# Uncut float32 scores for the first 14 head pairs, moved weight loads, and two orders of work instead of one, in a kernel of attention and a gated feed-forward layer

## The chip, the cores and the metric

The kernel runs on one core of a Trainium2 chip. The metric is device time in microseconds (us) of that core. The core has five queues that matter here: PE (TensorE, matmuls and weight loads), DVE (VectorE), ACT (ScalarE), POOL (GpSimd) and SP (SyncE, which here issues nearly all DMAs). Each runs its own instructions strictly in the order in which the program emits them, and waits at semaphores for the others.

## What is computed

Eight batches, twelve heads, 448 positions, head size 64. Attention with capped scores, then a feed-forward layer on its output with squared ReLU and a sigmoid gate.

```python
# attention, per head
scores = q @ k.T / sqrt(64)
scores = cap * tanh(scores / cap)
attn = exp(scores - max(scores))
attn = attn / (sum(attn) + 1e-9)
x = attn @ v                       # heads side by side: [8, 448, 768]
# feed-forward
x_prev = x shifted by one position
xk = mu_k * x + (1 - mu_k) * x_prev
xr = mu_r * x + (1 - mu_r) * x_prev
k = relu(xk @ w_k)                 # [8, 448, 1024]
v = k * k @ w_v
out = sigmoid(xr @ w_r) * v
```

The weights arrive as float64, in pairs of 32-bit words.

## The kernel before

**Two phases.** The first phase walks over the 48 head pairs (8 batches of 6 pairs) in 54 steps. The second walks over 28 chunks of 128 tokens and computes gate and output; it is nearly all matmuls (`chunk2`, L482, with `mm2`, L475). Only the first phase is touched by the change.

**A step of the first phase.** Step i does scores, tanh, exp and row sums (`red`, L255) of pair i, the product with the values (`V`, `values`, L234) of pair i-1, and the normalisation and mixing (`norm`, `mix_old`, `mix_new`, `x_high`, `x_low`) of pair i-2. Keys are cut in three groups of 128 (S0, S1, S2) and a rest of 64, which is done for two pairs at once in even steps (`L`, `tanhL`, `expL`, `redL`, `VL`). The row sums go through DRAM twice to be inverted and spread over partitions: `gather` (four small DMAs), `recip` on DVE, `rec_store` and `rec_load`; `norm` of the next step needs the result.

**Scores.** `scores` (L197) multiplies in three terms. `qk_high` rounds q and k to float32r on POOL, `qk_low` subtracts to get the rest, also float32r and on POOL (both at step i for pair i+2), and high*high, low*high and high*low are summed in PSUM. A float32 operand that is not cut is also possible: the rest of 64 keys (L216) and the product with the values (L241) use it; one float32 matmul is two matmul instructions in the trace. Score tiles have two buffers, so that a group waits until tanh has read the one before the last.

**Key products.** From step 7 on, each step has four places K (`kpart`, L323), with 7 key matmuls in each place of an even step and 5 in each of an odd step (`key_split`, L530), 48 in two steps. They need the mixed x of the pairs and the converted key weights. `relu` and `k_store` on ACT empty a finished group.

**Weights.** 44 pieces (16 of the key weight first) are loaded one per step (`weight_load`), and an extra one at `more` in steps 1, 3, 5, 7 and 9. ACT takes the absolute value at the end of the step (`weight_abs`), and in the next step DVE does five operations for each piece (`f`, `weight_rest`; L395 to L403), POOL adds (`weight_sum`, L410) and rounds, and DVE subtracts one step later (`weight_low`, L423, for pieces of the key weight).

**The order** is written out by hand, in one list for even and one for odd steps; a name in the list emits its instructions, so the list sets each engine's queue.

```python
EVEN = """gather load_v load_vl weight_load more weight_low S0 S1 V VL L S2 f f f f f weight_rest tanh0 exp0 red0
weight_sum tanh1 exp1 red1 norm recip rec_store K qk_high qk_low tanhL mix_old mix_new x_high x_low relu k_store
K expL redL relu k_store K K tanh2 exp2 red2 relu k_store weight_abs load_qk rec_load x_store weight_store"""
```

**The passage.** After step 48 the buffers of attention are freed, and the weights of the second phase (14 loads of `w_d`, L544, in three buffers) are loaded and cut while the last key products run.

## Time and profile before

| | us |
|---|---|
| median of 3 runs (lowest, highest) | 977.08 (975.99, 978.48) |
| profiled execution: its own time | 976.81 |
| profiled execution: span of instructions | 975.0 |
| PE busy | 931.0 (95%) |
| DVE busy | 633.5 (65%) |
| ACT busy | 487.8 (50%) |
| POOL busy | 291.7 (30%) |

Busy shares are means over stages that differ. Positions are us from the start of the span. In the slices of the span, PE is at six to eight tenths in the first three (75 us), and at nine or more in all but the last after that. The clock that TensorE was granted is written as a share of full speed: 1.00 is 2.4 GHz, and 0.5 is 1.2 GHz.

### The profile page before, as it was taken

To read this page: it belongs to the slowest core of one execution; us is meant where nothing else is said; L and a number is where in the kernel's file an instruction comes from. 1 tells how busy PE (TensorE), PEld (TensorE's weight loads), DVE (VectorE), ACT (ScalarE), POOL (GpSimd) and SP (SyncE) were. 2 spreads that over 40 slices of the span, in tenths; PEclk is the share of its full clock that TensorE was granted. 3 is DMA by queue.
4 is the path that set the end of the run, shared out by engine and by line. 5 is a ranking of instruction groups with operands and counts; after the bars stand their busy time and mean duration, and the time that the engine had idled before them with its cause. 6 is when DMAs were issued, how large, how long until landed. Compare 5 with 4: busy or idle time off the path is not lost.

```text
span 975.0 us, 14675 instructions
## 1 busy us (share of the span) xinstructions
PE 931.0 (95%) x5328; PEld 747.0 (77%) x5328; DVE 633.5 (65%) x1128; ACT 487.8 (50%) x578; POOL 291.7 (30%) x315
## 2 busy tenths in 40 slices
PE   6667899999999999999999999999999999999997
PEld 3224566666666666666667899999999999999997
DVE  5999887788877778776553685464464464465450
ACT  6767777887888888887773121221221221121120
POOL 4566565555555546554422300000000000000000
PEclk8778999999999999999999999999999999999999
DMA  4554555766766766664434752332232233233221
GB/s 156 160 155 150 181 159 184 220 209 193 217 185 192 222 201 191 199 191 147 142 125 146 251 156 84 87 109 80 83 108 83 82 109 90 73 109 93 71 71 36
DMA packets 124706, 138.88 MB, mean 142 GB/s; under 512 B 19664, under 2 KB 109776, under 8 KB 124624
## 3 DMA queue, kind: packets, MB, share of 16 engines
q1 hardware_dynamic: 115408, 123.16, 42.7%
q10 hardware_dynamic: 9216, 14.68, 4.0%
q8 instruction: 44, 0.72, 0.3%
q14 instruction: 38, 0.31, 0.1%
HBM read 92.64 MB, written 42.40 MB: 139 GB/s over the span
## 4 chain that ended last, share of the span: by engine, by line
PE 82%; DVE 9%; DMA 3%; ACT 3%; issue 1%; SPq 1%; POOL 1%; DVEq 0%; ACTq 0%; POOLq 0%
PE pvv L479 23%; PE kps L336 20%; PE pr L479 17%; PE pv L241 10%; PE s L204 9%; DVE r L257 2%; PE pv L250 2%; PE s L216 1%; DMA wst<-w_d 1%; ACT p L222 1%; DVE wt L395 1%; ACT p L232 1%; DMA sq<-r 1%; DVE wa L399 1%; ACT p_left L232 1%
## 5 line engine op out<-in xcount | busy, mean ns | idle before, releaser
L257 DVE TRANSPOSE_TENSOR_REDUCE r<-p 128x28 f32<-128x896 f32 x144 | 158.8, 1109 | 72.7 <-ACT p L232 72.0
L79 ACT CAST xh<-t 128x768 fp32r<-128x768 f32 x27 | 22.6, 837 | 309.5 <-DVE t L462 309.5
L222 ACT ACTIVATE p<-s,scl_t 128x896 f32<-128x896 f32 x144 | 143.3, 995 | 23.0 <-PE s L204 15.2
L232 ACT ACTIVATE p<-p,cap_t 128x896 f32<-128x896 f32 x144 | 150.0, 1042 | 3.9
L336 PE MATMUL kps<-xkh,wkh 128*128 128x448 f32 x384 | 143.5, 374 | 3.4 <-ACT ko L343 3.2
L494 DVE TENSOR_TENSOR o<-pvv,rsg 128x768 f32<-128x768 f32 (+1 forms) x29 | 27.0, 930 | 181.2 <-PE pvv L479 180.3
L336 PE MATMUL kps<-xkl,wkh 128*128 128x448 f32 x384 | 142.7, 372 | 0.2 <-POOL xkl L85 0.2
L336 PE MATMUL kps<-xkh,wkl 128*128 128x448 f32 x384 | 140.2, 365 | 0.0
L241 PE MATMUL pv<-p,rv 128*64 128x448 f32 x576 | 125.9, 574 | 2.0 <-DVE xk L301 2.0
L479 PE MATMUL pvv<-wvh,kl 128*128 128x384 f32 x448 | 115.0, 334 | 0.0
L479 PE MATMUL pvv<-wvh,kh 128*128 128x384 f32 x448 | 114.9, 334 | 0.0
L479 PE MATMUL pvv<-wvl,kh 128*128 128x384 f32 x448 | 114.9, 334 | 0.0
L85 POOL TENSOR_TENSOR qkl<-rqk,qkh 128x832 fp32r<-128x832 f32 x47 | 93.1, 1980 | 3.9
L204 PE MATMUL s<-qkh 64*128 64x448 f32 x288 | 65.2, 448 | 29.7 <-ACT p L222 20.1
L204 PEld LDWEIGHTS s<-qkh 64*128 64x128 f32 x288 | 27.8, 188 | 83.3 <-ACT p L222 31.6
L241 PEld LDWEIGHTS pv<-p,rv 128*64 128x64 f32 x576 | 38.7, 143 | 66.7 <-issue 56.4
L479 PE MATMUL pr<-wrh,xh 128*128 128x384 f32 x336 | 85.5, 335 | 1.7 <-POOL xh L75 1.0
L479 PE MATMUL pr<-wrh,xl 128*128 128x384 f32 x336 | 85.5, 335 | 1.0 <-DVE xl L470 1.0
L336 PEld LDWEIGHTS kps<-xkh,wkh 128*128 128x128 f32 x384 | 72.1, 188 | 18.2 <-ACT ko L343 6.8
L479 PE MATMUL pr<-wrl,xh 128*128 128x384 f32 x336 | 85.2, 334 | 0.0
L410 POOL TENSOR_TENSOR wsq<-wa,wsq 128x384 f32<-128x384 f32 x44 | 44.4, 1010 | 129.8 <-DVE wsq L403 113.2
L336 PEld LDWEIGHTS kps<-xkl,wkh 128*128 128x128 f32 x384 | 72.1, 188 | 12.8 <-issue 6.8
(75 smaller groups left out, 1552.0 us busy)
## 6 DMA issues: line engine op xcount, KB each, us to landing
rqk<-qk SPq DMA_DIRECT2D x47, 448.0 KB
k_d<-ko ACTq DMA_DIRECT2D x64, 224.0 KB
kr<-k_d SPq DMA_DIRECT2D x28, 512.0 KB
x_d<-x SPq DMA_DIRECT2D x48, 224.5 KB
r<-rec_d SPq DMA_DIRECT2D x96, 112.0 KB
out<-o SPq DMA_DIRECT2D x27, 384.0 KB
xc<-x_d SPq DMA_DIRECT2D x24, 387.0 KB
rv<-v SPq DMA_DIRECT2D x48, 192.0 KB
```

Of the source, the lines that this page charges most:

```text
L79: self.nc.scalar.copy(out, x)
L85: {"p": self.nc.gpsimd, "v": self.nc.vector}[e].tensor_sub(*a)
L204: nc.tensor.matmul(s[:, h, 0:S], qk[a][p, k], qk[b][p, 0:S], start=(n == 0), stop=(n == 2))
L222: self.nc.scalar.activation(p32, self.S.pop((i, g))[:, :, 0:S], AF.Tanh, scale=self.scl_t)
L232: self.nc.scalar.activation(p32, p32, AF.Exp, scale=1.0 if self.maxima else self.cap_t)
L241: nc.tensor.matmul(pv[p, 0:S], v[:, g, h, :], ph[:, h, :], start=(g == 0), stop=False)
L250: self.nc.tensor.matmul(self.PV[i + p][o, 0:S], v[HALF[p], h, :], ph[HALF[p], h, :], start=False, stop=True)
L257: self.nc.vector.tensor_reduce(out=r1[:, :, 3 if g == "L" else g], in_=self.P32[i, g].rearrange("p h (b k) -> p (h b) k", k=32), axis=mybi ...
L336: nc.tensor.matmul(self.kps[fc][:, 0:S], w, m[:, dc, :], start=first, stop=last)
L410: {"p": self.nc.gpsimd, "v": self.nc.vector}[e].tensor_add(sq, f(a), sq)
L479: self.nc.tensor.matmul(ps[:, m, 0:HN], a[:, c, :], w[:, c, m * HN:m * HN + HN], start=(c == 0 and part == 0), stop=(c == n - 1 and part = ...
L494: nc.vector.tensor_mul(o[:, q], pv[:, q, 0:HN], rs[:, q])
```

## The change

The scores of pairs 0 to 13 are computed from the loaded float32 q and k, in one term; `qk_high` and `qk_low` fall away for these pairs. The five extra weight pieces are loaded in steps 1, 7, 8, 9 and 10. There are four lists instead of two: one pair for steps 0 to 13 and one for the others. The number of key matmuls per place stays as it was (the constants `KE`, `KO`, `KT` have the old values). In the maxima path, which runs only for a large cap, the same terms are used. `raw` and `QK` are no longer popped, which moves no work, and there are assertions on the order of key products.

```diff
+RAW = 14
+SW = 14
+MORE = (1, 7, 8, 9, 10)
+KFIRST = 28
+KE, KO, KT = (7, 7, 7, 7), (5, 5, 5, 5), 8
...
-EVEN = """gather load_v load_vl weight_load more weight_low S0 S1 V VL L S2 f f f f f weight_rest tanh0 exp0 red0
-weight_sum tanh1 exp1 red1 norm recip rec_store K qk_high qk_low tanhL mix_old mix_new x_high x_low relu k_store
-K expL redL relu k_store K K tanh2 exp2 red2 relu k_store weight_abs load_qk rec_load x_store weight_store"""
-ODD = """gather load_v weight_load more weight_low S0 S1 V S2 f f f f f weight_rest tanh0 exp0 red0
-weight_sum tanh1 exp1 red1 norm recip rec_store K qk_high qk_low tanh2 mix_old mix_new x_high x_low relu k_store
-K exp2 red2 relu k_store K K relu k_store weight_abs load_qk rec_load x_store weight_store"""
+START_EVEN = """gather weight_load load_v load_vl more load_qk weight_low S0 S1 K V VL L weight_rest f norm f tanh0 exp0
+qk_high weight_sum tanh1 exp1 relu k_store f recip red0 qk_low tanhL K S2 mix_old mix_new x_high x_low red1
+tanh2 relu expL redL exp2 k_store K K red2 f f weight_abs relu k_store rec_store rec_load x_store
+weight_store"""
+START_ODD = """gather more load_qk load_v weight_load f f f S0 S1 V S2 f f weight_low K tanh0 relu exp0 norm red0
+weight_rest weight_sum tanh1 recip rec_store qk_high tanh2 mix_old mix_new x_high qk_low x_low k_store exp2 K
+red2 relu exp1 red1 k_store K K relu weight_abs k_store weight_store x_store rec_load"""
+EVEN = """weight_load gather load_vl load_v load_qk weight_rest weight_low f S0 S1 V VL L S2 f f tanh1 tanh0 exp1 exp0
+qk_high weight_sum norm recip x_store more K qk_low tanhL relu mix_old red1 mix_new x_high x_low k_store K
+expL relu tanh2 redL f f red0 exp2 red2 k_store K K relu k_store weight_abs rec_store rec_load weight_store"""
+ODD = """gather more weight_store load_v weight_load f weight_rest S0 S1 V S2 weight_low f K relu tanh0 k_store exp0
+red0 qk_high weight_sum tanh1 f norm f recip load_qk rec_store K exp1 red1 f tanh2 mix_old mix_new x_high
+qk_low x_low exp2 relu k_store weight_abs K K relu k_store red2 rec_load x_store"""
...
+    def factors(self, i):
+
+        if i < RAW:
+            return (self.raw[i],), ((0, 0),)
+        return self.QK[i], ((0, 0), (1, 0), (0, 1))
+
     def scores(self, i, g):
-        nc, qk = self.nc, self.QK[i]
+        nc = self.nc
+        qk, terms = self.factors(i)
         s = self.ps_s.tile([P, 2, 512], F32, name="s")
         k = slice(S + g * P, S + (g + 1) * P)
 
-        for n, (a, b) in enumerate(((0, 0), (1, 0), (0, 1))):
+        for n, (a, b) in enumerate(terms):
             for h, p in enumerate(HALF):
-                nc.tensor.matmul(s[:, h, 0:S], qk[a][p, k], qk[b][p, 0:S], start=(n == 0), stop=(n == 2))
-        if g == 2:
-            self.QK.pop(i)
+                nc.tensor.matmul(s[:, h, 0:S], qk[a][p, k], qk[b][p, 0:S], start=(n == 0), stop=(n == len(terms) - 1))
         self.S[i, g] = s
...
-        for op in (EVEN if even else ODD).split():
+        for op in ((START_EVEN if even else START_ODD) if i < SW else EVEN if even else ODD).split():
...
-                if 0 <= j < NPAIR:
+                if 0 <= j < NPAIR and not (j < RAW and op in ('qk_high', 'qk_low')):
                     getattr(self, name.get(op, op))(j, *g)
...
-                if i in (1, 3, 5, 7, 9):
+                for _ in range(MORE.count(i)):
                     self.weight_load()
...
             self.load_qk(0)
-            self.qk_high(0, "v")
-            self.qk_low(0, "v")
             self.consts(cpool)
             self.init_sums(cpool)
             self.load_qk(1)
-            self.qk_high(1)
-            self.qk_low(1)
             self.load_qk(2)
```

## Rows read from the trace of the kernel before

**Rows 1.** The page's busy time of the engines over the whole span: us, share, instructions.

```profile
PE 931.0 (95%) x5328; PEld 747.0 (77%) x5328; DVE 633.5 (65%) x1128; ACT 487.8 (50%) x578; POOL 291.7 (30%) x315
```

**Rows 2.** Busy time of each engine in seven stretches. Columns: the stretch, its length, then for each engine busy us and number of instructions, the granted TensorE clock, the DMA engines' busy share and GB/s. The bounds are starts of S0 on PE: of step 5, 6 and 7 (51.30, 64.80, 75.10), of step 8, 10, 12 and 14 (90.85, 114.84, 137.28, 158.60); 504.00 lies in step 47, 557.65 is the end of the last key product and 576.65 the start of the second chunk's gate products.

```profile
51.30:64.80 13.50, 7.61 (x30) 3.27 (x32) 12.34 (x22) 7.86 (x9) 7.66 (x10) 0.62 0.45 134
64.80:75.10 10.30, 6.84 (x48) 2.58 (x46) 9.84 (x17) 8.43 (x10) 6.72 (x7) 1.00 0.54 175
90.85:114.84 23.99, 21.31 (x125) 13.92 (x124) 21.41 (x36) 17.40 (x22) 14.51 (x18) 1.00 0.56 170
114.84:137.28 22.44, 21.71 (x125) 13.84 (x124) 19.91 (x32) 16.17 (x21) 12.56 (x16) 1.00 0.55 174
137.28:158.60 21.32, 21.28 (x127) 14.15 (x128) 17.85 (x30) 17.63 (x23) 13.11 (x13) 1.00 0.63 193
158.60:504.00 345.40, 345.24 (x2031) 226.49 (x2032) 256.62 (x409) 280.51 (x331) 182.12 (x189) 1.00 0.61 187
557.65:576.65 19.00, 16.25 (x89) 15.12 (x88) 15.59 (x25) 2.26 (x3) 4.48 (x4) 1.00 0.52 152
```

**Rows 3.** PE in order of time in an odd step of the steady stretch, from its S0 (255.52) to that of the next step (264.42). Columns: start, duration, instruction, count.

```profile
255.52 0.47 PE L204 MATMUL s<-qkh 64*128 64x448 f32 x2
...
256.94 2.48 PE L241 MATMUL pv<-p,rv 128*64 128x448 f32 x12
259.35 0.47 PE L204 MATMUL s<-qkh 64*128 64x448 f32 x2
...
260.16 0.47 PE L336 MATMUL kps<-xkh,wkh 128*128 128x448 f32 x1
...
264.42 0.47 PE L204 MATMUL s<-qkh 64*128 64x448 f32 x2
```

**Rows 4.** DVE in order of time in steps 4 and 5: the last weight piece of step 4, red0 and red1 of that step, norm, the three operations of recip (only the first shown), mix_new, redL, then weight_low for two pieces, a weight piece and two reds.

```profile
49.59 1.19 DVE L395 TENSOR_SCALAR wt<-wsq 128x384 f32<-128x384 f32 x1
...
52.87 2.10 DVE L257 TRANSPOSE_TENSOR_REDUCE r<-p 128x28 f32<-128x896 f32 x2
54.89 0.58 DVE L286 TENSOR_TENSOR x<-pv,r 128x448 f32<-128x448 f32 x1
55.40 0.59 DVE L270 TENSOR_REDUCE sr<-sq 32x28 f32<-32x448 f32 x1
...
56.51 0.64 DVE L301 SCALAR_TENSOR_TENSOR xk<-x,mu_k,pv 128x448 f32<-128x448 f32 x1
57.14 1.11 DVE L257 TRANSPOSE_TENSOR_REDUCE r<-p_left 128x28 f32<-128x896 f32 x1
...
60.15 0.98 DVE L423 TENSOR_TENSOR wkl<-wsq,wkh 128x384 fp32r<-128x384 f32 x2
61.05 0.35 DVE L395 TENSOR_SCALAR wt<-wsq 128x384 f32<-128x384 f32 x1
...
63.29 2.10 DVE L257 TRANSPOSE_TENSOR_REDUCE r<-p 128x28 f32<-128x896 f32 x2
```

**Rows 5.** DVE's instructions from 23.9 to 139.6 us, grouped by line: count, busy us and mean ns of one, then idle time before them and what ended it.

```profile
L257 DVE TRANSPOSE_TENSOR_REDUCE r<-p 128x28 f32<-128x896 f32 x31 | 33.5, 1100 | 6.8 <-ACT p L232 6.6
L395 DVE TENSOR_SCALAR wt<-wsq 128x384 f32<-128x384 f32 x15 | 12.2, 816 | 0.5
L423 DVE TENSOR_TENSOR wkl<-wsq,wkh 128x384 fp32r<-128x384 f32 x16 | 9.9, 641 | 0.0
...
L397 DVE TENSOR_SCALAR wa<-wt 128x384 uint32<-128x384 uint32 x15 | 6.4, 428 | 0.5
...
L257 DVE TRANSPOSE_TENSOR_REDUCE r<-p_left 128x28 f32<-128x896 f32 x5 | 5.6, 1114 | 1.0 <-ACT p_left L232 1.0
```

**Rows 6.** POOL: the page's group of qk_low over the whole span (count, busy us, mean ns, idle time before), and the instruction in order of time at the weight piece that stands first in rows 4.

```profile
L85 POOL TENSOR_TENSOR qkl<-rqk,qkh 128x832 fp32r<-128x832 f32 x47 | 93.1, 1980 | 3.9
...
49.56 1.00 POOL L410 TENSOR_TENSOR wsq<-wa,wsq 128x384 f32<-128x384 f32 x1 [2.27 <-DVE wsq L403]
```

**Rows 7.** Who waited for whom from 20 to 140 us, on ACT and on PE: us in total, times, longest.

```profile
ACT pv L296 <- DVE x L286: 21.7, 9, 4.3
...
PE s L204 <- ACT p L222: 18.8, 9, 5.9
```

**Rows 8.** DVE in order of time: the last row sum of step 1 and that of step 11.

```profile
22.85 1.11 DVE L257 TRANSPOSE_TENSOR_REDUCE r<-p 128x28 f32<-128x896 f32 x1 [1.36 <-ACT p L232]
...
138.56 1.11 DVE L257 TRANSPOSE_TENSOR_REDUCE r<-p 128x28 f32<-128x896 f32 x1
```

**Rows 9.** The start (DVE and ACT in order of time), and a product with the values on PE in step 5.

```profile
5.60 0.15 DVE L95 RECIPROCAL scl_t<-cap_t 128x1 f32<-128x1 f32 x1
...
6.89 1.01 ACT L222 ACTIVATE p<-s,scl_t 128x896 f32<-128x896 f32 x1
...
59.48 4.69 PE L241 MATMUL pv<-p,rv 128*64 128x448 f32 x12
```

**Rows 10.** The end of attention: SP's issues in order of time (the store of the inverted sums of pair 46, the gather of pair 47, the first three weight loads of the second phase), and the DVE operation that waits for that gather.

```profile
517.49 0.33 SPq L277 DMA_DIRECT2D rec_d<-rs  x1
...
520.65 2.46 SPq L266 DMA_DIRECT2D sq<-r  x4
...
528.78 1.64 SPq L544 DMA_DIRECT2D wst<-w_d  x3
...
524.43 0.61 DVE L270 TENSOR_REDUCE sr<-sq 32x28 f32<-32x448 f32 x1 [1.26 <-DMA sq<-r]
```

More of the change, by code (lines that the diff above doesn't have):

```diff
@@ L175, in row_maxima @@
     def row_maxima(self, i):
-        nc, qk, raw = self.nc, self.QK[i], self.raw[i]
+        nc, raw = self.nc, self.raw[i]
+        qk, terms = self.factors(i)
         m = self.up.tile([S // 4, 8], F32, name="m", bufs=1)
@@ L185, in row_maxima @@
                 q = slice(c * S // 4, (c + 1) * S // 4)
-                for n, (a, b) in enumerate(((0, 0), (1, 0), (0, 1))):
-                    nc.tensor.matmul(o[:, 0:KM], qk[b][t, q], qk[a][t, S:QM], start=(n == 0), stop=(n == 2))
+                for n, (a, b) in enumerate(terms):
+                    nc.tensor.matmul(o[:, 0:KM], qk[b][t, q], qk[a][t, S:QM], start=(n == 0), stop=(n == len(terms) - 1))
                 nc.tensor.matmul(o[:, KM:S], raw[t, q], raw[t, QM:QA], start=True, stop=True)
@@ L195, in row_maxima @@
             nc.sync.dma_start(M[:, h], self.max_d[h:h + 1, :].to_broadcast([P, S]))
+    def factors(self, i):
+        if i < RAW:
+            return (self.raw[i],), ((0, 0),)
+        return self.QK[i], ((0, 0), (1, 0), (0, 1))
     def scores(self, i, g):
-        nc, qk = self.nc, self.QK[i]
+        nc = self.nc
+        qk, terms = self.factors(i)
         s = self.ps_s.tile([P, 2, 512], F32, name="s")
         k = slice(S + g * P, S + (g + 1) * P)
-        for n, (a, b) in enumerate(((0, 0), (1, 0), (0, 1))):
+        for n, (a, b) in enumerate(terms):
             for h, p in enumerate(HALF):
-                nc.tensor.matmul(s[:, h, 0:S], qk[a][p, k], qk[b][p, 0:S], start=(n == 0), stop=(n == 2))
-        if g == 2:
-            self.QK.pop(i)
+                nc.tensor.matmul(s[:, h, 0:S], qk[a][p, k], qk[b][p, 0:S], start=(n == 0), stop=(n == len(terms) - 1))
         self.S[i, g] = s
@@ L213, in scores_left @@
         for p in range(2):
-            raw = self.raw.pop(i + p)
+            raw = self.raw[i + p]
             for h, t in enumerate(HALF):
@@ L310, in x_low @@
         self.sub(e, xl[:, hp, :], self.xk, f(xh[:, hp, :]))
+        self.xdone.add((b, hp))
     def x_store(self, i):
@@ L329, in kpart @@
             xh, xl = self.XK[b]
+            assert (b, dc) in self.xdone and (fc, dc // 3) in self.wdone
             first, last = (dc, t) == (0, 0), (dc, t) == (ND - 1, 2)
@@ L415, in weight_sum @@
                 self.copy(e, hi, sq)
-                self.w_low.append((lo, sq, hi))
+                self.w_low.append((lo, sq, hi, (fc, d)))
             else:
@@ L421, in weight_low @@
     def weight_low(self):
-        for lo, sq, hi in self.w_low:
+        for lo, sq, hi, n in self.w_low:
             self.nc.vector.tensor_sub(lo, sq, f(hi))
+            self.wdone.add(n)
         self.w_low = []
@@ L532, in key_split @@
         n, total, out = 0, B * NF * ND * 3, {}
-        for c in range(28, NSTEP * 4):
+        for c in range(KFIRST, NSTEP * 4):
             i = c // 4
-            w = min(8 if i >= NPAIR else 5 if i % 2 else 7, total - n)
+            w = min(KT if i >= NPAIR else (KO if i % 2 else KE)[c % 4], total - n)
             out[i, c % 4] = (n, n + w)
@@ L558, in run @@
         self.order = self.key_order()
+        self.xdone, self.wdone = set(), set()
         self.ksplit = self.key_split()
```

## The prediction, made before the changed kernel ran

> **What bounds the kernel now.** I read the busy shares first, then busy time by stretch, then each engine in order of time. PE is busy for 931 of 975 us [rows 1], so what can be won is where PE isn't. From 158.6 to 504 us it works 345.24 of 345.40 us at clock 1.00 [rows 2]. Both new lists for later steps keep PE's own order (S0 S1 V VL L S2 and four K; S0 S1 V S2 and four K), so these 34 steps should cost the same. The second phase isn't touched. What is left is steps 0 to 13 and the passage at the end of attention.
>
> In steps 2 to 11 DVE sets the pace. Its last row sum of step 1 ends at 23.9 us and that of step 11 at 139.6 [rows 8]: 115.7 us, in which it waits only 6.8 + 1.0 us [rows 5]. Others wait for it: `mix_old` on ACT 21.7 us for `norm`, and behind ACT the scores on PE 18.8 us [rows 7]. PE is idle 2.7 of 24.0 us in steps 8 and 9 and 0.7 of 22.4 in 10 and 11; in 12 and 13 it is full [rows 2].
>
> **DVE's account.** Start-to-start times [rows 4]: two row sums 2.02, so 1.02 each (redL about the same); norm 0.51; recip's three operations 1.11; mix_new 0.63; weight_low 0.45 for a piece; a weight piece 2.24 when nothing disturbs it (61.05 to 63.29). An even step without weights is 4 x 1.02 + 0.51 + 1.11 + 0.63 = 6.33, an odd one 5.31. Steps 2 to 11 before: five of each, 58.2; 15 pieces, 33.6; 15 weight_low, 6.75: 98.55 us of work.
>
> The rest is disturbance. L395 takes 0.816 in the mean against 0.35 alone [rows 4, 5]: 15 x 0.466 = 7.0. L423 has 9.9 - 16 x 0.52 = 1.6 too much (0.52 estimated from the pair of 0.98), L397 15 x (0.428 - 0.36) = 1.0. Together 9.6. The first row of rows 4 shows how: L395 of the second piece takes 1.19, and POOL's weight_sum runs from 49.56 to 50.56 [rows 6]. With the 7.8 of waiting: 98.55 + 9.6 + 7.8 = 115.95, against 115.7 read.
>
> The Trainium skill (SBUF — State Buffer, Who interferes with whom) says that VectorE and GpSimd share a port pair as an exclusive lock, which whichever starts first keeps for its whole instruction. Rows 4 and 6 agree. By that rule alone the disturbance after the change would be the 3.6 us of the lower bound below, and the time 1.0 us less than I forecast.
>
> **The change on DVE.** Extra pieces move: steps 3 to 7 have one each, 8 to 11 two each. Steps 2 to 7 are then 3 x 6.33 + 3 x 5.31 + 7 x 2.24 + 7 x 0.45 = 53.75; steps 8 to 11 2 x 6.33 + 2 x 5.31 + 8 x 2.24 + 7 x 0.45 = 44.35. Sum 98.1: moving the pieces takes away nothing, since all 16 key pieces are still due by step 12. The gain must come from four other terms.
>
> - *Start.* DVE's cast and subtraction for pair 0 fall away, and the constants that the first tanh (6.89) needs start at 5.60 behind them [rows 9]. At most 1.6 us earlier; but uncut scores and V are slow at the low clock there. I take 0.9 (bounds 0 and 1.6).
> - *Disturbance.* POOL loses qk_low, 1.98 us a pair [rows 6], and the rounding ahead of it. In new odd steps norm and red0 (1.5 us) lie between the two pieces, in even ones they still follow each other: steps 2, 8 and 10, 1.2 us each, 3.6. Bounds 3.6 and 9.6; I take 4.6, as x_low may still meet a piece.
> - *Waits.* Norm now lies ahead of most row sums, so ACT's mix_old isn't held. But the gather of the even list waits for red1, the last DVE work of the odd step; from its issue to recip is 3.8 us (520.65 to 524.43) [rows 10], and weight_low, one piece and norm cover 3.2 to 3.65. That leaves up to 0.6 in steps with one piece, 2.4 in all with the odd ones. Bounds 2.4 and 12 (each of ten steps as badly joined as the worst, 1.2); I take 5.5 against 7.8.
>
> Behind the gather on SP stand the loads of v, of q and k for pair i+3 and of the weights. A weight piece is needed one step later, q and k three steps later, so they have at least 7 us.
>
> End of DVE's step 11: 23.0 + 98.1 + 4.6 + 5.5 = 131.2 instead of 139.6, 8.4 earlier.
>
> **The change on PE.** An odd steady step is 8.90 us: S0 and S1 1.42, V 2.41, S2 0.81, 20 key matmuls 4.26 [rows 3]. Uncut scores aren't in the trace. The nearest row is V: 12 float32 instructions for six matmuls in 2.41, so 0.80 for a group of scores with its two halves side by side, against 0.61 to 0.81 in three terms. Bounds 0.61 (as cut) and 1.56 (half clock, by V's 4.69 in rows 9). At 0.80, fewer changes between number formats counted, an odd step gains 0.35. In the even start list two K stand among float32 work: two more changes, at 0.2 to 0.4 each (estimated from 256.94 - 255.52 = 1.42 for two groups of 0.61), so 1.15 in all. Steps 12 and 13, PE's own, go from 21.3 to 22.8. Steps 8 to 11 on PE: 2 x 9.25 + 2 x 13.57 = 45.6; if PE starts step 8 where DVE ends step 7 (23.0 + 53.75 + 5 of waits and disturbance = 81.8, my choice), it could end step 11 at 127.4. DVE with PE ahead of it by 2.3 as now (137.28 against 139.6) allows 128.9. So DVE still decides, narrowly. Step 14 starts at 128.9 + 22.8 = 151.7 instead of 158.6: 6.9 us won.
>
> POOL's cutting for pairs 0 to 13 hid behind DVE; its time is worth nothing by itself.
>
> **The passage.** The second phase's weight loads start at 528.78, behind a chain on SP: rec_store of pair 46 at 517.49, gather of 47 at 520.65, recip at 524.43 [rows 10]. In the new odd list recip stands ahead of red1, one or two row sums earlier, so the chain can move forward by up to 2.2. It ends in 19.0 us with PE idle 2.75 [rows 2], which limits it. I take 0.6 (bounds 0 and 2.2).
>
> **Sum.** Against the profiled execution, 975.0 span and 976.8 time (median 977.08, 0.3 more): -6.9 - 0.6 = -7.5, so 969.3 us.
>
> **Rivals.**
> *Given back (0.14).* DVE's work to step 11 is the same 98 us. If disturbance and waits stay at 9.6 and 7.8, because two pieces in each of steps 8 to 11 make norm late, DVE ends step 11 at 138.5, and with 1.5 more on PE nothing is won: 976 to 977. For it: work unchanged. Against: most of the disturbance is L395's 7.0, and POOL is emptier. This is also the case that the uncut scores do nothing.
> *PE at half clock (0.07), slower.* Place: steps 1 to 6. In step 5 the clock was 0.62 and V took 4.69, in step 6 1.00 [rows 2, 9], after a wait of up to 5.9 us [rows 7]. The two products of the rest, L and VL, are what an even step has more than an odd one beside 8 key matmuls: 21.32 - 2 x 8.90 - 8 x 0.21 = 1.8 [rows 2, 3]. At full clock two steps are 6 x 0.80 + 2 x 2.41 + 1.8 = 11.4 us of PE work, at half clock 6 x 1.56 + 2 x 4.69 + 3.5 = 22.2, and DVE gives 6.33 + 5.31 + 2 x 2.69 + 1.5 of waits and disturbance = 18.5. PE decides once (18.5 - 11.4) / (22.2 - 11.4) = 0.66 of its work is at the low clock. If all is, steps up to 7 win nothing, steps 8 to 11 take 44.35 + 2.4 + 2 = 48.7 against 46.4, 12 and 13 1.5 more: about 980. Against: an engine that is never idle isn't seen at the low clock here (1.00 in all full stretches).
> The Trainium skill (TensorE: Matmul & The Clock Gate, HAM oscillation) describes this rival: waits between bursts of matmuls put the clock back to half. Step 5 agrees.
> *A gap in the steady stretch (0.07), slower.* Late lists put tanh1 ahead of tanh0 and a relu ahead of tanh0 in odd steps. If PE waits 0.6 us in each of 17 pairs of steps, the gain is gone and more: 979. Against: ACT works 280.5 of 345.4 us there [rows 2], and PE has 4.3 us of key products after S2 [rows 3].
> *PE decides (0.10).* All four terms at their good ends, step 14 at 149 and the passage 2.2 earlier: 963 to 965.
>
> **How the numbers follow.** Forecast 0.62 (alone 964.5 to 974). Under 964 lies a third of the last rival, over 976 the two slower ones and some of the first: range 964 to 976. About 0.3% (2.9 us) can be told from no change. Faster: 0.62 + 0.10 + 0.04 of the first rival; slower: 0.14; the same: 0.10.
>
> **What would show it.** Step 14's S0 on PE near 152; DVE's last row sum of step 11 near 131; L395's mean from 23 to 131 us near 0.5; mix_old's wait for norm well under 21.7; the four instructions of an uncut group in 0.8 us; a steady pair of steps still 21.1 to 21.3; weight loads of the second phase earlier than step 14 alone gives. I am wrong if DVE idles more than 8 us up to step 11, if the clock stays at half through steps 2 to 6, or if PE shows gaps after step 14.

## The result, and the profile of the changed kernel

The changed kernel takes 981.8 us (median; 979.3 to 987.0) against 977.1: ratio 1.0051, 95% interval 1.0028 to 1.0074. It is slower; 969.3 had been forecast, and the range ended at 976. The profiled execution has a span of 979.8 us, 4.8 more than before. The starts of the products with the values (V) on PE divide these 4.8 us:

| | before | after | difference |
|---|---|---|---|
| first V of step 14 | 159.88 | 153.90 | -5.98 |
| from there to the first V of step 48 | 358.76 | 370.72 | +11.97 |
| from there to the end | 456.37 | 455.23 | -1.14 |

So the start gave nearly what was expected of it (6.0 us of 6.9), and the steady stretch, which had been costed at nothing, took twice that.

In the listing of the changed kernel the lines stand lower: L395, L397 and L423 are now L415, L417 and L443, V (L241) is L259, recip's first operation (L270) L288, norm (L286) L304, mix_new (L301) L319, and the issues on SP (L266, L277, L282) L284, L295 and L300.

**The start.** The last two row sums of step 11 on DVE, and on PE S0 and S1 of step 12 and the first scores of step 14, in order of time:

```profile
132.27 2.10 DVE L275 TRANSPOSE_TENSOR_REDUCE r<-p 128x28 f32<-128x896 f32 x2
...
129.77 1.77 PE L224 MATMUL s<-rqk 64*128 64x448 f32 x8
...
152.17 0.47 PE L224 MATMUL s<-qkh 64*128 64x448 f32 x2
```

Two lines of DVE from 19 to 134.4 us (columns as in [rows 5]):

```profile
L443 DVE TENSOR_TENSOR wkl<-wsq,wkh 128x384 fp32r<-128x384 f32 x15 | 10.8, 740 | 0.0
L415 DVE TENSOR_SCALAR wt<-wsq 128x384 f32<-128x384 f32 x15 | 7.2, 478 | 2.0 <-ACT wsq L395 1.8
```

Waits from 20 to 140 us, on ACT and on PE (as in [rows 7]):

```profile
ACT pv L314 <- DVE x L304: 3.1, 3, 1.5
PE pv L259 <- DMA rv<-v: 12.9, 4, 4.5
PE s L224 <- ACT p L240: 3.9, 6, 1.0
```

S0 of step 14 starts at 152.17 (forecast 151.7; 158.60 before [rows 2]). L415 takes 0.478 us in the mean, about the 0.5 expected, where it took 0.816 [rows 5]. `mix_old` waits 3.1 us for norm and PE 3.9 us behind ACT, where it was 21.7 and 18.8 [rows 7]. One wait is new: PE waits 12.9 us for the load of v.

**The steady stretch.** Busy time from S0 of step 14 to 504 us (columns as in [rows 2]):

```profile
152.17:504.00 351.83, 342.21 (x1989) 224.56 (x1990) 281.55 (x407) 268.13 (x325) 182.82 (x188) 1.00 0.58 183
```

Waits from 155 to 515 us in the changed kernel: all of PE's, SP's load of the inverted sums for their store, and recip on DVE for its gather.

```profile
PE pv L259 <- DVE xk L319: 6.8, 7, 2.1
PE kps L356 <- ACT ko L363: 1.6, 2, 1.0
PE s L224 <- ACT p L240: 0.5, 3, 0.2
...
SPq L300 <- DMA rec_d<-rs: 88.2, 34, 4.2
...
DVE sr L288 <- DMA sq<-r: 37.5, 25, 2.7
```

The same stretch of the kernel before, in which PE waited for nothing:

```profile
SPq L282 <- DMA rec_d<-rs: 37.7, 34, 2.5
...
DVE sr L270 <- DMA sq<-r: 16.0, 13, 2.3
```

The sizes of SP's transfers in the changed kernel, over the whole span (count, KB each; the gather sq<-r is four of them):

```profile
rqk<-qk SPq DMA_DIRECT2D x47, 448.0 KB
...
x_d<-x SPq DMA_DIRECT2D x48, 224.5 KB
...
rv<-v SPq DMA_DIRECT2D x48, 192.0 KB
...
w<-wv SPq DMA_DIRECT2D x16, 384.0 KB
...
sq<-r SPq DMA_DIRECT2D x192, 14.0 KB
...
rec_d<-rs SPq DMA_DIRECT2D x48, 3.5 KB
```

PE was idle 0.16 us in this stretch [rows 2]; now it is idle 9.6 us of 351.8. (From V of step 14 to V of step 48 it is idle 9.4 us and busy 361.3 instead of 358.6, which together are the 12.) Seven times V waits for `mix_new`, which frees the PSUM tile that V writes. Behind that, the small transfers have become slow: the 3.5 KB store of the inverted sums is awaited 88.2 instead of 37.7 us, 1.5 us more in each of 34 steps, and recip waits for its gather in 25 of 33 steps, 37.5 us in all, where it did in 13 of 34, 16.0 us.

ACT waits for transfers too, at `weight_abs`, from 155 to 515 us, in the changed kernel and then in the kernel before:

```profile
ACT wsq L395 <- DMA w<-wv: 11.9, 7, 2.2
ACT wsq L395 <- DMA w<-wr: 11.2, 5, 3.6
...
ACT wsq L375 <- DMA w<-wr: 1.6, 2, 1.2
```

So the weight loads themselves come late as well: 23.1 us of waiting in 12 steps, where it was 1.6 in 2.

Two steps of the changed kernel on SP in order of time (an odd one, then an even one; start, duration, instruction):

```profile
304.01 0.53 SPq L169 DMA_DIRECT2D rv<-v  x1
304.63 0.38 SPq L387 DMA_DIRECT2D w<-wv  x1
305.11 0.38 SPq L164 DMA_DIRECT2D rqk<-qk  x1
306.46 0.34 SPq L295 DMA_DIRECT2D rec_d<-rs  x1
310.66 1.12 SPq L300 DMA_DIRECT2D r<-rec_d  x2
...
312.99 2.44 SPq L284 DMA_DIRECT2D sq<-r  x4
...
316.57 0.43 SPq L164 DMA_DIRECT2D rqk<-qk  x1
317.10 0.38 SPq L332 DMA_DIRECT2D x_d<-x  x1
318.75 0.33 SPq L295 DMA_DIRECT2D rec_d<-rs  x1
321.80 1.12 SPq L300 DMA_DIRECT2D r<-rec_d  x2
...
324.12 2.44 SPq L284 DMA_DIRECT2D sq<-r  x4
```

The instructions on DVE that belong to them (recip's first operation and mix_new), and the V that waits:

```profile
305.24 0.61 DVE L288 TENSOR_REDUCE sr<-sq 32x28 f32<-32x448 f32 x1 [0.16 <-DMA sq<-r]
317.53 0.61 DVE L288 TENSOR_REDUCE sr<-sq 32x28 f32<-32x448 f32 x1 [2.53 <-DMA sq<-r]
...
327.91 0.61 DVE L288 TENSOR_REDUCE sr<-sq 32x28 f32<-32x448 f32 x1 [0.40 <-DMA sq<-r]
330.03 0.62 DVE L319 SCALAR_TENSOR_TENSOR xk<-x,mu_k,pv 128x448 f32<-128x448 f32 x1
...
330.71 2.48 PE L259 MATMUL pv<-p,rv 128*64 128x448 f32 x12 [0.88 <-DVE xk L319]
```

The reader is to see a ring in these rows. Recip on DVE (305.24) ends in the transpose that the store waits for (306.46); the load of the inverted sums needs the store landed (310.66, 4.20 us later, with v, weights, and q and k issued ahead of the store, 1,024 KB in the 2.5 us before it); the gather of the next pair stands behind that load on SP (312.99, its four parts issued by 315.43); recip of the next pair waits for it (317.53, 2.53 us of idle DVE). Then the ring goes round again: store 318.75, load 321.80 (3.05 us later; v, q and k, and x_store stand ahead, 864 KB), gather 324.12, recip 327.91. Two rounds take 327.91 - 305.24 = 22.67 us. Two of PE's steps take 358.8 / 17 = 21.1. Where the ring takes longer than PE's two steps, everything behind recip on DVE comes later from step to step, `mix_new` with it, until V has to wait for it (330.71, 0.88 us). The ring itself is not new; before, recip found its gather landed in 21 of 34 steps, so that it had room left. In the changed kernel the last weight load is issued at 423.13. From V of step 14 to V of step 40 (441.5) two steps take 22.1 us, and from there to V of step 46 (505.0), without weight loads, 21.2.

### The profile page after: what moved, and what is told of

It reads as the page before. It is cut to its first block, busy times and chain, and to the rows that moved or that the text cites. A ratio compares the mean times of both kernels' runs of the same rounds, so it can differ in the third digit from the quotient of the medians.

```text
span 979.8 us, 14498 instructions
## 1 busy us (share of the span) xinstructions
PE 937.7 (96%) x5244; PEld 737.8 (75%) x5244; DVE 652.7 (67%) x1126; ACT 478.1 (49%) x578; POOL 255.4 (26%) x289
## 4 chain that ended last, share of the span: by engine, by line
PE 52%; DVE 21%; DMA 17%; SPq 5%; ACT 3%; issue 2%; POOL 0%; DVEq 0%; ACTq 0%; POOLq 0%
PE pvv L500 23%; PE pr L500 17%; DVE r L275 7%; DMA sq<-r 6%; PE kps L356 5%; SPq L284 4%; PE pv L259 3%; DMA rec_d<-rs 3%; DVE wt L415 3%; DMA r<-rec_d 2%; PE s L224 2%; DVE sr L288 2%; DVE wa L417 2%; DVE xk L319 1%; DMA w<-wr 1%
## 5 line engine op out<-in xcount | busy, mean ns | idle before, releaser
L275 DVE TRANSPOSE_TENSOR_REDUCE r<-p 128x28 f32<-128x896 f32 x144 | 153.4, 1076 | 13.4 <-ACT p L250 13.1
L240 ACT ACTIVATE p<-s,scl_t 128x896 f32<-128x896 f32 x144 | 141.1, 995 | 17.6 <-PE s L224 14.6
L250 ACT ACTIVATE p<-p,cap_t 128x896 f32<-128x896 f32 x144 | 147.3, 1039 | 2.4
L259 PE MATMUL pv<-p,rv 128*64 128x448 f32 x576 | 127.2, 579 | 20.0 <-DMA rv<-v 13.2
L259 PEld LDWEIGHTS pv<-p,rv 128*64 128x64 f32 x576 | 39.5, 143 | 87.6 <-issue 53.7
L500 PEld LDWEIGHTS pvv<-wvh,kh 128*128 128x128 f32 x448 | 81.0, 188 | 0.0
L500 PEld LDWEIGHTS pvv<-wvh,kl 128*128 128x128 f32 x448 | 81.0, 188 | 0.0
L500 PEld LDWEIGHTS pvv<-wvl,kh 128*128 128x128 f32 x448 | 81.0, 188 | 0.0
L356 PEld LDWEIGHTS kps<-xkh,wkl 128*128 128x128 f32 x384 | 72.2, 188 | 7.3 <-issue 2.0
```

What stands on the lines that cost most here:

```text
L240: self.nc.scalar.activation(p32, self.S.pop((i, g))[:, :, 0:S], AF.Tanh, scale=self.scl_t)
L250: self.nc.scalar.activation(p32, p32, AF.Exp, scale=1.0 if self.maxima else self.cap_t)
L259: nc.tensor.matmul(pv[p, 0:S], v[:, g, h, :], ph[:, h, :], start=(g == 0), stop=False)
L275: self.nc.vector.tensor_reduce(out=r1[:, :, 3 if g == "L" else g], in_=self.P32[i, g].rearrange("p h (b k) -> p (h b) k", k=32), axis=mybi ...
L356: nc.tensor.matmul(self.kps[fc][:, 0:S], w, m[:, dc, :], start=first, stop=last)
L500: self.nc.tensor.matmul(ps[:, m, 0:HN], a[:, c, :], w[:, c, m * HN:m * HN + HN], start=(c == 0 and part == 0), stop=(c == n - 1 and part = ...
```

## The experiments

A step's order is a list of operations, so each experiment but one (`qk_on_act`) is an edit of lists or of the steps of the extra pieces. "Old" and "new" lists are those of the kernel before and of the change. The table has the median times, the intervals of their ratios to the kernel before, V of step 14 and the time from there to V of step 48 in the profiled execution, and from 155 to 515 us the two waits just shown: SP's for the store (us), and recip's for the gather (us, and in how many of some 33 steps). The kernel before ran beside each group, at 976.9 to 977.9, so that medians of different groups can differ by some 1 us without cause.

| kernel | us | ratio to before, 95% | V(14) | V(14) to V(48) | store | gather |
|---|---|---|---|---|---|---|
| before | 977.1 |  | 159.9 | 358.8 | 37.7 | 16.0 / 13 |
| after | 981.8 | 1.0028 to 1.0074 | 153.9 | 370.7 | 88.2 | 37.5 / 25 |
| late_old | 972.6 | 0.9951 to 0.9973 | 153.8 | 360.3 | 42.7 | 12.7 / 12 |
| late_old_v_first | 975.3 | 0.9970 to 0.9996 | 156.8 | 360.6 | 39.4 | 16.3 / 15 |
| raw_only | 977.2 | 0.9974 to 0.9998 | 159.9 | 358.8 | 43.4 | 12.3 / 12 |
| raw_more | 975.7 | 0.9961 to 0.9986 | 157.0 | 358.8 | 39.3 | 12.2 / 13 |
| new_work_old_dma | 971.2 | 0.9903 to 0.9947 | 154.9 | 358.8 | 29.7 | 7.5 / 11 |
| old_work_new_dma | 991.5 | 1.0077 to 1.0170 | 152.0 | 379.8 | 97.3 | 41.1 / 27 |
| qk_late | 987.7 | 1.0097 to 1.0149 | 154.3 | 377.3 | 40.9 | 60.6 / 31 |
| late_old_qk_early | 997.7 | 1.0176 to 1.0228 | 153.0 | 387.9 | 112.1 | 35.8 / 26 |
| qk_on_act | 978.0 | 0.9983 to 1.0037 | 153.5 | 370.3 | 51.8 | 40.0 / 26 |
| odd_new_dma | 973.5 | 0.9936 to 0.9971 | 153.7 | 365.7 | 66.2 | 14.1 / 17 |
| even_new_dma | 970.1 | 0.9915 to 0.9964 | 150.7 | 358.8 | 54.3 | 24.6 / 19 |
| even_store_back | 975.4 | 0.9966 to 0.9992 | 153.8 | 364.5 | 67.8 | 31.2 / 18 |
| even_gather_first | 993.9 | 1.0149 to 1.0183 | 152.5 | 385.3 | 116.0 | 38.8 / 29 |
| even_qk_last | 973.8 | 0.9960 to 0.9987 | 153.8 | 362.7 | 55.1 | 29.4 / 15 |
| odd_store_first | 972.0 | 0.9924 to 0.9957 | 153.3 | 360.4 | 52.7 | 17.6 / 18 |
| all_old_dma | 966.0 | 0.9846 to 0.9901 | 150.3 | 358.8 | 33.5 | 10.2 / 13 |

**Start or late lists?** late_old takes the whole change but uses the old lists from step 14 on.

```diff
 START_EVEN, START_ODD: as changed
-EVEN = """weight_load gather load_vl load_v load_qk ...   (new)
+EVEN = """gather load_v load_vl weight_load more ...      (old; ODD likewise)
```

> The lists for steps 14 and later are those of the kernel before; steps 0 to 13 stay as changed. If the loss of 12.1 us between V of step 14 and V of step 48 sits in the late lists, that stretch takes 358 to 360 us again (358.6 before, 370.7 after), the time falls to 968 to 972 us, and step 14 still starts near 152 us. If the loss comes with the start (a state that steps 0 to 13 leave behind, such as weights or row sums that stay late), the stretch keeps 366 us or more and the time is over 976.

Measured: 972.6 us, 0.6 above what was expected. V of step 14 is where it was in the changed kernel, and the stretch behind it goes back to 360.3. The loss sits in the late lists.

**Transfers or compute?** The late lists changed two things at once: where the operations of the engines stand, and where SP's issues stand. Theory A puts the loss on the issues, theory B on the compute. Two kernels cross them.

```diff
 new_work_old_dma: order of compute new, issues as in the old lists (here the end of ODD)
-recip load_qk rec_store K ... red2 rec_load x_store
+recip rec_store K ... red2 load_qk rec_load x_store weight_store
 old_work_new_dma: order of compute old, issues as in the new lists
```

> The late lists (steps 14 on) keep the changed order of compute, but every operation that issues a transfer stands where the old late lists had it: the gather and the loads of v and of weights at the front, the store of the row sums right behind the reciprocal, and at the end the load of q and k, the load of the reciprocals, the stores. The start lists are those of the change. Theory A (the transfers' order costs the steady stretch its 12.1 us: bulk loads stand ahead of small transfers in the queue) expects 971 to 975 us, V(14) to V(48) at 360 to 364 us, and waits of the load of reciprocals for their store of 34 to 42 us in all. Theory B (the order of compute costs it: mix_new and the abs come later than PE wants them) expects 979 to 983 us, V(14) to V(48) at 368 to 372 us, with the V matmuls waiting for mix_new 5 to 8 us in all.

> The mirror image: the late lists keep the old order of compute, but every operation that issues a transfer stands as in the changed late lists (the load of q and k ahead of the store of the row sums in odd steps, the weight and v loads ahead of or behind the gather as the change has them, the store and the load of reciprocals late in even steps). Theory A expects at least 979 us, up to 990, with V(14) to V(48) at 368 us or more. Theory B expects 971 to 976 us and V(14) to V(48) at 359 to 364 us.

Measured: 971.2 and 991.5 us, the second 1.5 above its range. With the old order of compute the new issues cost 991.5 - 972.6 = 18.9 us, with the new order 981.8 - 971.2 = 10.6. Theory A holds; B's sign is the other way: the new compute is 1.4 us better with the old issues (2.2 when each is set against the kernel before of its own group) and 9.7 with the new ones. In new_work_old_dma PE has no wait in the whole stretch, and V(14) to V(48) is 358.8, as before the change: that the new lists leave PE's 34 steps alone was true of their compute.

**Which wait in the ring?** qk_late moves the load of q and k, which in the changed lists stands ahead of the store, behind the load of the inverted sums; late_old_qk_early does the reverse to the old lists; qk_on_act leaves all places and lets ACT issue that load, so that it goes by the other queue.

```diff
 qk_late, both late lists:
-... load_qk ... rec_store ... rec_load ...
+... rec_store ... rec_load load_qk ...
 late_old_qk_early:
-recip rec_store K ... load_qk rec_load x_store
+recip load_qk rec_store K ... rec_load x_store
 qk_on_act, from step 14 on:
-self.nc.sync.dma_start(t[:, c], self.qk[i // NP, i % NP][:, c])
+(self.nc.scalar if i >= SW + 3 else self.nc.sync).dma_start(t[:, c], self.qk[i // NP, i % NP][:, c])
```

> The changed kernel with one edit: in the two late lists load_qk stands behind rec_load instead of ahead of rec_store. Theory A (the 448 KB of q and k are ahead of the 3.5 KB of rec_store in the DMA queue; SP then holds at rec_load, and the next gather, recip and all row sums behind recip are late): rec_load's wait for rec_store falls from 2.7 us to under 1.6 us in the mean, and the stretch from V of step 14 to V of step 48 loses at least 8 of its 12.1 us too many, so 968 to 974 us. Theory B (the late lists put row sums behind recip on DVE and weight operations beside POOL's cutting, whatever the DMA order): the stretch stays within 3 us of 370.7 and the time at 978 to 983.

> Old late lists, with load_qk moved from behind the last weight_abs to just ahead of rec_store, in steps 14 and later. Theory A: rec_load's wait for rec_store rises from 1.1 us (before) to 2.5 us or more; as the row sums stand ahead of recip in these lists, part of it stays hidden, so the time is 1 to 10 us over that of late_old. Theory B: rec_load's wait may grow, but the time stays within 1.5 us of late_old.

> The changed kernel with all lists as they are; from step 14 on the 448 KB load of q and k is issued by ACT instead of SP, at the same place of the list, so that it goes to the other DMA queue. Theory A1 (what delays the row sums' store is the bulk load ahead of it in the same queue) expects SP's waits of the load of reciprocals for that store to fall from 88 us to 45 to 65 in the steady stretch (the weight load ahead of the gather in even steps stays), and the time to fall to 970 to 978 us. Theory A2 (the engines that move the data are shared, whichever queue a load came by) expects the waits to stay at 80 us or more and the time at 979 to 985. ACT pays under 0.1 us for each issue, 34 of them, unless a buffer is late.

Measured: 987.7, 997.7 and 978.0 us. The waits from 155 to 515 us, of SP for the store and of recip for its gather, in qk_late:

```profile
SPq L300 <- DMA rec_d<-rs: 40.9, 33, 2.5
...
DVE sr L288 <- DMA sq<-r: 60.6, 31, 4.0
```

And in qk_on_act:

```profile
SPq L300 <- DMA rec_d<-rs: 51.8, 34, 3.3
...
DVE sr L288 <- DMA sq<-r: 40.0, 26, 4.4
```

In qk_late the wait for the store fell from 88 to 41 us, as theory A said, and the time rose by 6 us, which it had not said: the 448 KB now stand right ahead of the next gather, whose wait went from 37.5 to 60.6 us, in 31 steps. The ring has two landings of small transfers in it, and a bulk load ahead of either lengthens it. In late_old_qk_early one load moved ahead of the store costs 25 us against late_old; 1 to 10 had been expected. In qk_on_act the store's wait fell to 51.8 us, into the range of theory A1, but recip still waited 40.0 us in 26 steps and the time fell by only 3.8 us, with intervals that overlap: it lies between A1 and A2, at the edge of A1's range, with the steady stretch at 370.3 as in the changed kernel. So it isn't the queue alone. The Trainium skill (DMA: Bandwidth & Descriptors, Queues, rings and completion order) says that SP and ACT each have a ring on each of the same 16 engines, and that an engine takes turns between rings. The run agrees: the store no longer waits behind the load (51.8 for 88.2 us), but recip's waits for the gather don't get shorter (40.0 for 37.5). How the packets of the two queues took turns isn't shown by these rows.

**Which places?** Two kernels have the new issues in one list only; four undo one move in the changed kernel.

```diff
 odd_new_dma: EVEN with the old issues;  even_new_dma: ODD with the old issues
 even_store_back:
-norm recip x_store more K ... weight_abs rec_store rec_load weight_store
+norm recip rec_store x_store more K ... weight_abs rec_load weight_store
 even_gather_first:
-weight_load gather load_vl load_v load_qk
+gather load_vl load_v weight_load load_qk
 even_qk_last:
-load_vl load_v load_qk ... rec_store rec_load weight_store
+load_vl load_v ... rec_store load_qk rec_load weight_store
 odd_store_first:
-recip load_qk rec_store K
+recip rec_store load_qk K
```

> Late lists in the changed order of compute; the transfers of even steps stand as in the old even list, those of odd steps as in the changed odd list (the load of q and k right ahead of the store of the row sums, extra pieces and weight stores ahead of the load of v). If the loss of 10.6 us sits in the odd steps, where the 448 KB load stands right ahead of the 3.5 KB store, this takes 978 to 983 us; if it sits in the even steps, 970 to 974 us; if both carry a part, 974 to 978.

> The mirror image: the transfers of odd steps stand as in the old odd list, those of even steps as in the changed even list (a weight load ahead of the gather, the load of q and k at the front, the store of the row sums only at the end of the step, right ahead of the load that needs it). If the loss sits in the odd steps, 970 to 974 us here; if in the even steps, 978 to 983; if both carry a part, 974 to 978. My money is on a part for each, the larger on the odd steps.

> The changed kernel with one edit: in the late even list the store of the row sums stands right behind the reciprocal again, as the old list had it, instead of at the end. By the trace SP reaches the store early in either place and waits there for the reciprocal's transpose, so the place in the list should not be its cause: my theory expects 980 to 983 us and the same waits, 80 to 92 us. If the late place in the list were what holds it, the time would fall by 3 us or more, to 979 or less.

> The changed kernel with one edit: in the late even list the 384 KB weight load stands behind the gather and the loads of v, as in the old list, instead of ahead of the gather. If a bulk load right ahead of the 14 KB gathers is a part of the loss, DVE's waits of the reciprocal for the gather fall from 37.5 us to 20 to 30 and the time to 976 to 980 us. If only the loads ahead of the store count, 980 to 983.

> The changed kernel with one edit: in the late even list the 448 KB load of q and k stands behind the store of the row sums instead of at the front, two transfers ahead of it. If the bulk load shortly ahead of the small store is the cause in even steps too, the even steps' wait of the load of reciprocals for the store falls from 2.7 to under 1.5 us, the sum from 88 to 60 to 70, and the time to 972 to 978 us. If the place of that load in even steps is indifferent, 980 to 983; if it then delays the next step's gather instead, as it did when both loads were moved, 983 to 988.

> The changed kernel with one edit: in the late odd list the store of the row sums and the 448 KB load of q and k right ahead of it change places. If that load costs by being right ahead of the store, the odd steps' wait falls from 3.5 to 4.2 us to about 1, the sum from 88 to 45 to 60, and the time to 970 to 976 us, since even steps alone with the changed places cost nothing. If the load then takes its price from the next transfers, 977 to 983.

Measured: the odd list alone costs 2.3 us (973.5 against 971.2, with intervals that overlap), the even list alone nothing (970.1), both together 10.6. A sum of costs doesn't explain that; room that is used up does: two rounds of the ring may take 21.1 us, and the first lengthening is free until then. But the ring isn't the only way by which late transfers reach PE. In odd_new_dma V never waits for `mix_new`, and the only wait of PE from 155 to 515 us is another:

```profile
PE s L224 <- ACT p L240: 6.5, 5, 2.3
```

ACT, which computes the tanh that these scores wait for, idles 29.9 us before `weight_abs` until some transfer has landed, where it was 1.6 before and 3.3 in new_work_old_dma. No experiment separates this path from the ring; in the changed kernel V's waits for `mix_new` are 6.8 of PE's 8.9 us. In the same way each of three single moves undone in the changed kernel brings most of it back: 975.4, 973.8 and 972.0 us. odd_store_first, where the expectation had it at 970 to 976 with 45 to 60 us of waits, gave 972.0 and 52.7; even_qk_last 973.8 (972 to 978) and 55.1 (60 to 70).

Two of these expectations missed altogether. even_store_back was to change nothing, since SP reaches the store early wherever it stands. But the edit also puts the store ahead of x_store, and those 224 KB were what stood between recip and the store: 67.8 instead of 88.2 us, 975.4 us. even_gather_first was to help and cost 12 us. On SP, in order of time:

```profile
323.91 0.38 SPq L387 DMA_DIRECT2D w<-wv  x1
324.33 0.43 SPq L164 DMA_DIRECT2D rqk<-qk  x1
324.85 0.38 SPq L332 DMA_DIRECT2D x_d<-x  x1
325.33 0.37 SPq L295 DMA_DIRECT2D rec_d<-rs  x1
331.14 1.12 SPq L300 DMA_DIRECT2D r<-rec_d  x2
```

The gather has no weight load ahead of it now, but the 384 KB have moved behind it, right ahead of q and k, x_store and the store. The store is issued at 325.33, and the load that needs it at 331.14, 5.81 us later.

**The start, part by part.** raw_only has the uncut scores alone (old lists in all steps, pieces in steps 1, 3, 5, 7, 9), raw_more the moved pieces as well; late_old_v_first is late_old with the load of v moved ahead of the extra pieces and of q and k in the odd start list, because of the 12.9 us that PE waits for it.

```diff
 raw_only:  RAW = 14, MORE = (1, 3, 5, 7, 9), all four lists old
 raw_more:  RAW = 14, MORE = (1, 7, 8, 9, 10), all four lists old
 late_old_v_first, START_ODD:
-gather more load_qk load_v weight_load f f f
+gather load_v more load_qk weight_load f f f
```

> As the kernel with uncut scores and extra pieces and the old lists, but the key weight pieces stay in steps 1, 3, 5, 7 and 9. My theory prices the pieces' move at nothing to 1 us: 971 to 976 us, within 1.5 us of that kernel, and step 14's first scores within 1.5 us of it. If the moved pieces matter, the two differ by 2 us or more.

> The old even and odd lists in all steps, with only the scores of the first 14 pairs from uncut float32 and the extra key weight pieces in steps 7 to 10. If the start's gain (step 14's first scores at 152.17 us instead of 158.60) comes from the uncut scores, these stand at 151.5 to 154.5 here and the time is 971 to 975 us. If it comes from the start lists, they stand at 156 to 159 and the time is 975 to 978 us.

> Old late lists, and in the odd start list load_v stands right behind gather, ahead of load_qk. V of even start steps waited for the load of v 13.2 us in five steps (the changed kernel). If these waits are on the path, step 14 starts 1 to 5 us earlier than in late_old, and the time is 1 to 5 us less. If DVE's account alone sets the pace of steps 2 to 11, as in the prediction, the waits go elsewhere and the time is within 1 us of late_old.

Measured: 977.2, 975.7 and 975.3 us. V of step 14 starts at 159.86 with the uncut scores alone (before: 159.88), at 157.04 with the pieces, at 153.84 with the start lists (late_old). Of the 6.0 us the scores by themselves gave nothing, pieces on top of them 2.8, lists 3.2; by the median times it is 0.7 for the scores (977.2 against 977.9 of the kernel before beside it), 1.5 and 3.1 (2.3 when each is set against the kernel before of its own group). raw_only was expected at 971 to 976 and missed that. (In the thirteen kernels of the table that share the changed start, V of step 14 lies between 150.7 and 154.9, so one profile's start is good to some 2 us; the medians carry this.) DVE by line in raw_only from 23.9 to 139.6 us, as in [rows 5] (a line of this listing is one lower than in the changed kernel's):

```profile
L442 DVE TENSOR_TENSOR wkl<-wsq,wkh 128x384 fp32r<-128x384 f32 x15 | 11.1, 767 | 0.0
L414 DVE TENSOR_SCALAR wt<-wsq 128x384 f32<-128x384 f32 x14 | 9.1, 651 | 0.5
```

L414 fell from 0.816 to 0.651 us, which is 14 x 0.165 = 2.3 us won, but L442 rose from 0.641 to 0.767, 1.9 us lost: the disturbance went down in one operation and up in another. The trace shows with what: every long one of L442 (1.22 to 1.24 us) runs while POOL does `x_low`, which before met the weight piece three times (1.23 to 1.31); the long ones of L414 that are left (1.19) run beside `weight_sum`, as before. With the load of v first (late_old_v_first) PE's waits for v went to 2.0 us, but the time rose by 975.3 - 972.6 = 2.7 us, V of step 14 with it, outside both ranges of the expectation, and V waits for `mix_new` up to 3.9 us instead. What the load costs where it stands isn't settled by it.

**The version that beats both.** all_old_dma has the changed order of compute and the old places of all issues, in the start lists too.

```diff
 START_EVEN:
-gather weight_load load_v load_vl more load_qk weight_low ... f recip red0 ... rec_store rec_load x_store weight_store
+gather load_v load_vl weight_load more weight_low ... f recip rec_store red0 ... load_qk rec_load x_store weight_store
 START_ODD:
-gather more load_qk load_v weight_load f ... weight_store x_store rec_load
+gather load_v weight_load more f ... load_qk rec_load x_store weight_store
 EVEN, ODD: as in new_work_old_dma
```

> The changed order of compute in all steps, and in all steps the transfers at the places of the old lists, in the start lists too: the load of v ahead of the extra weight pieces and of the load of q and k, the store of the row sums right behind the reciprocal. If the 13 us that the start's V matmuls wait for their v are on the path, V of step 14 comes 2 to 4 us ahead of the 153.9 us and the time is 967 to 970 us. If they are covered by DVE, whose 98 us of work sets the start, nothing or a little is lost, as it was when the load of v alone was moved ahead (156.8): 970 to 974 us.

Measured: 966.0 us (963.2 to 968.1), ratio 0.9873 (0.9846 to 0.9901); 1.0 us beyond the good end of what was expected. By the medians the start's issues are worth 971.2 - 966.0 = 5.2 us; V of step 14 comes 4.6 us ahead of new_work_old_dma's in the profiles. On SP in a step of the steady stretch, in order of time:

```profile
313.16 0.38 SPq L387 DMA_DIRECT2D w<-wv  x1
...
315.76 0.34 SPq L295 DMA_DIRECT2D rec_d<-rs  x1
316.19 0.33 SPq L164 DMA_DIRECT2D rqk<-qk  x1
317.06 1.13 SPq L300 DMA_DIRECT2D r<-rec_d  x2
...
320.60 2.45 SPq L284 DMA_DIRECT2D sq<-r  x4
```

And the recips on either side of it on DVE:

```profile
314.56 0.59 DVE L288 TENSOR_REDUCE sr<-sq 32x28 f32<-32x448 f32 x1
324.33 0.61 DVE L288 TENSOR_REDUCE sr<-sq 32x28 f32<-32x448 f32 x1 [0.33 <-DMA sq<-r]
```

The store goes first and the load of q and k behind it; the load of the inverted sums follows 1.30 us after the store (2.34 in the next step), where it took 3.05 and 4.20. The recip at 314.56 didn't wait for its gather at all, the next one 0.33 us.

## Why the prediction was wrong

*The step that failed* is this one: "Both new lists for later steps keep PE's own order [...], so these 34 steps should cost the same." They cost 12.0 us more. PE's order is indeed kept, and where only compute was reordered the 34 steps take 358.8 us to a tenth (new_work_old_dma). But the lists also order SP, and the prediction looked at SP's moves once and only at what the moved loads themselves need: "A weight piece is needed one step later, q and k three steps later, so they have at least 7 us." For q and k that held: PE waits for none of these loads in the steady stretch. For the weights it didn't: `weight_abs` on ACT reads a piece in the same step that loads it, and its waits for weight loads went from 1.6 to 23.1 us. And the sentence leaves out the small transfers behind the loads, which have no time to lose. What should have been costed is the ring: from recip through the store's landing, the load's issue, the gather's issue and landing to the next recip. Of the trace before, [rows 10] show a part of it (3.8 us from the gather's issue to recip), used for the start alone.

*The rival "A gap in the steady stretch"* had the place and, at 979, nearly the price (12.0 us of loss against the 10 or so that it implies). Its cause, the order of tanh and relu on ACT, was wrong: PE waits 0.5 us for ACT's tanh there and 6.8 for DVE's `mix_new`, and in new_work_old_dma, with the same order on ACT, PE doesn't wait at all. With 0.07 it was held for far too unlikely.

*The start* came out nearly right as a sum and not by its parts; that the errors cancelled is luck. S0 of step 14: 151.7 forecast, 152.17 measured; S0 of step 12 128.9 and 129.77; steps 12 and 13 22.8 and 22.4. But DVE ended step 11 at 134.4, not at 131.2. It had ended step 1 at 21.9, where 23.0 was forecast: 2.0 us won, above the 1.6 given as that term's bound. Its work was as counted, 98.1. The disturbance was 15 x (0.478 - 0.35) + 0.6 for L417 + 2.6 for L443 (15 x 0.740, less 1.2 for one of step 12 and 14 x 0.52), 5.1 in all (4.6 taken). The waits were underrated: norm for PE 3.6 and the load 1.0, recip for its gather 2.2, L415 for ACT 1.8, 8.6 against 5.5. Together 133.7 of the 134.4. It cost little because S0 of step 12 needs no longer follow DVE's end so closely: it starts 4.6 us ahead of it, where 2.3 had been taken over from before.

The reason given for *Disturbance*, that POOL loses `qk_low`, was wrong. Before, no long L395 or weight_low up to step 12 runs beside `qk_low`; they run beside `weight_sum` and `x_low`, which stay. L415 is long three times in the changed kernel, in steps 2, 8 and 10 as foreseen, and what came on top is weight_low beside `weight_sum` (1.35 us at 37.89). That moving pieces "takes away nothing" was wrong by 1.5 to 2.8 us.

*Uncut scores on PE:* 0.80 us a group had been taken; two groups take 1.77 with the last one's end (the row of 129.77), so this term stood.

*The passage* gained 1.1 us against 0.6, within its bounds.

*PE at half clock* did show: V runs 4.62 and 4.75 us in steps 2 and 4, at a granted clock of 0.53 and 0.50, after waits of 4.46 and 3.23 us for its v, as 4.69 in [rows 9]. DVE still set the pace up to step 11, as the prediction argued; what the low clock cost isn't separated by a run. *Given back* and *PE decides* didn't come about. Of the three signs of being wrong that the prediction named, two showed: DVE's waits up to step 11 are over 8 us, and PE has gaps after step 14.

What stays open: why the pieces' move gains 1.5 to 2.8 us (no run moved them alone), how much of the 12.9 us for v is on the path (all issues put back won 5.2 us, the load of v alone lost 2.7), and why even_new_dma, odd_store_first and even_qk_last, alike in their waits for the store (52.7 to 55.1 us), lose 0, 1.6 and 3.9 us in the steady stretch (PE doesn't wait in the first, waits 1.5 us for `mix_new` in the second, and 3.4 of 3.6 us for ACT's tanh in the third). How the loss divides between the ring and ACT's waits for late weights is open too. The stretches are those of one profiled execution each.

## What to carry to other kernels

When an in-order queue issues both bulk loads and small transfers with a result that something waits for, cost a reordering by what comes to stand behind each bulk load, and not only by how early the load itself is needed; and look up which operation needs it first. Look for a ring through that queue (a store, a load that needs it landed, the next gather behind it, the operation that feeds the next store), add up one round, and set it against the time of the loop's pacing engine: the difference is the room, moves are free until it is used up, and then every round pays. An engine's unchanged order says nothing about an engine that feeds it.

## What the runs showed of the hardware

From the issue of the 3.5 KB store to that of the load that needs it landed, it takes longer the more bulk bytes the same queue was given just before. In steps 14 to 38, by the KB that SP issued in the 2.6 us ahead of the store: 1.29 to 1.34 us behind none (7 steps of the kernel before), 2.72 to 3.24 behind 864 and 2.85 to 4.64 behind 1,024 (8 and 9 steps of the changed kernel, medians 2.99 and 3.76), 4.80 to 5.86 behind 1,312 (10 steps of even_gather_first, median 4.99). The groups overlap, so the bytes aren't all that counts: behind 384 KB (8 steps of all_old_dma) it is 1.28 to 3.11.

Sending the bulk load by ACT's queue cut the waits for that store from 88 to 52 us and left the waits for the gather at 40. And taking `qk_low`, 1.98 us a pair [rows 6], and the rounding off POOL moved POOL's disturbance of DVE more than it ended it (raw_only): one DVE operation fell by 0.165 us, another rose by 0.126.
